# Two MLP layers behind attention: layer 1 of the first half batches cut into two halves of the inner columns

## The chip, the core and the metric

One core of a Trainium2 chip runs the whole program. The metric is the time of one execution on the device in microseconds (us): the median of three runs is 1666.7 us (1664.54 to 1667.3).

## What is computed

Attention with packing, then two gated layers over the 4608 tokens (8 batches of 576, 512 features). The weights come as 64-bit floats, q, k, v and p as 32-bit ones.

```
p_packed = sm_attn(p, k, v)                # 8 batches, 8 heads, 32 packed rows
out      = sm_attn(q, p_packed, p_packed)  # 576 rows per batch
x  = out as [4608, 512]
h  = x @ w_in1                             # 2048 inner columns
g  = (a0 + a1 h + a2 h^2 + a3 h^3) / (1 + |b0||h| + |b1| h^2 + 1e-6)
x2 = g @ w_out1                            # layer 1
h  = x2 @ w_in2;  g = h cos(h)
y  = g @ w_out2                            # layer 2
```

## The kernel before

**Stages.** Attention runs in 16 units (`attention`, a unit is one batch and four heads): loads of p, k, q and v, PE transposes (`trans`, `turned`), scores (`scores`, L500, twice a unit), soft-max on DVE, ACT and POOL, the packing product (`pack`). The packed rows (`keep_pack`) and the attention weights (`keep_attn`) go to DRAM. Layer 1 doesn't form `out`: `m_prod` (L695) multiplies packed rows with `w_in1` into M, per batch, half of the columns and group of heads, and `m_hi`, `m_lo` split M into two parts; `a2_load`, `a2_hi`, `a2_lo` do the same for the attention weights of a half batch (288 tokens).

**Items.** Layer 1 is 128 items: for each of 16 half batches c, eight items i of 256 inner columns. An item is 12 matmuls of `front` (L740) into a PSUM slot b2, some twelve operations for g (ACT: `absolute`, `lin`, `slope`, `log`, `inverse`, `upper`; DVE: `cubic` twice, `over` twice, `ratio`, `lower`; POOL: `denom`), and 24 matmuls of `back` (L777), six into each of four accumulators. After the eighth item `done1` (L786) copies the four to the tile ob and `x_out` stores them. Layer 2 is 144 items: nine chunks of 512 tokens, 16 items each, with `x_load`, `x_hi`, `x_lo` for the operands.

**Weights.** `convert` loads 128 rows of 64-bit words into raw and makes 32-bit values of them: `w_exp`, `w_low` on ACT, `w_abs` (L369), `w_join` (L379) on DVE, and for w_out a split by `w_hi` (ACT) and `w_lo` (POOL).

**What sets the order.** All engines' queues are fixed when the program is built. A planner (`Plan.order`) takes the steps with their costs, keys and slots and puts out one list; a step's key is its due time plus a number for its kind from the table `WANTED`. Slots say how many tiles of a kind live at once:

```
("T", "ep", ("T0", "T1", "T2", "T3")),
...
*((nm, "ld", tuple(f"{nm}_in{i}" for i in range(3))) for nm in "pkqv"),
SLOTS["tr"] = ["b2_0", "b2_1", "b3"]
```

Steps that use DVE's port together with POOL's (`SHARED`: `over`, `ratio`, `lower`, `rounded`, `clipped`, `w_abs`, `w_join`, `x_lo`) are kept apart from POOL's steps: the plan never runs one beside the other, and POOL waits for the last one before it. The pools of layer 1 (`sl2` for M, `a2p`, `ep` for T, U, V) lie in memory that the loads of attention (`ld`) leave, and gh, gl, ob, the accumulators and `wo1` in what its other tiles (`tp`) leave, so the last items' tiles wait for the end of attention (`open_left`, `open_right`). All loads and stores but the last ones go out from SP, in order.

Of the kernel before, what the change touches and what calls it, by code (L numbers as in the profile page):

```python
# [22 lines left out]
class Step:  # L23
    __slots__ = ("eng", "busy", "ns", "key", "fn", "args", "new", "objs", "deps", "outs",
                 "left", "ready", "start", "end", "kb", "n", "slots", "port", "behind", "ins")


class Plan:
# [14 lines left out]
        "a2_hi": -487, "a2_lo": 16, "a2_load": -116, "absolute": -171, "back 0": 868,  # L43
        "back 1": 414, "clipped": -39, "copied k": 50, "copied q": 379, "cosine": 427,
        "cubic 0": 2184, "cubic 1": 373, "denom": -324, "done1": -240, "done2": 222, "doubled": 65,
        "exp1": 12, "exp2": 366, "exp_copied": 1828, "front 0": -75, "front 1": 28, "inverse": -39,
        "keep_attn": -193, "keep_out": -663, "keep_pack": 344, "less_max2": -839, "lin 0": -40,
        "lin 1": -157, "load k": -100, "load p": 127, "load q": -16, "load v": -216, "log": 1940,
        "lower 0": -199, "lower 1": -193, "m_hi": 303, "m_lo": -7, "m_load": -209, "m_prod": -122,
        "max1": 209, "max2": -574, "open_left": 194, "open_right": -121, "over 0": 590,  # L50
        "over 1": 442, "pack": -397, "packed": 485, "ratio": 235, "recip1": 303, "recip2": -376,
        "reduced 0": 499, "reduced 1": 387, "rounded": -296, "scaled2": -170, "scores 0": -545,
        "scores 1": 7, "slope": 61, "store": 293, "sum2": -213, "taken p": 487, "taken pp": -300,
        "times": 372, "trans k": 320, "trans q": -206, "turn2": 432, "turn_back": 314,
        "turn_exp": 342, "turned p": 160, "turned pp": 85, "upper 0": -564, "upper 1": 392,
# [5 lines left out]
        "w_low 1 i": 264, "w_low 1 o": 185, "x_hi": 547, "x_lo": -435, "x_load": 274,  # L61
        "x_out": -308,
    }
    RATE = 262.0
    SHARED = ("over", "ratio", "lower", "rounded", "clipped", "w_abs", "w_join", "x_lo")

    def __init__(self, slots, mixed):
        self.slots_of, self.mixed = slots, mixed
# [4 lines left out]
    def add(self, eng, busy, key, fn, *args, tail=0, r=(), w=(), new=(), after=(), kb=0):  # L73
        key += self.WANTED.get(self.kind(fn.__name__, args), 0)
        s = Step()
        s.eng, s.busy, s.ns, s.key, s.fn, s.args, s.kb = eng, busy, busy + tail, key, fn, args, kb
# [41 lines left out]
    def order(self):  # L118
# [5 lines left out]
        slot_free = {x: 0 for xs in self.slots_of.values() for x in xs}  # L124
# [24 lines left out]
        while len(done) < len(self.steps):  # L149
# [15 lines left out]
            if s.kb:  # L165
                bus = max(bus, a + 600) + s.kb * 1024 / self.RATE
                s.end = bus + 1400
            else:
                s.end = a + s.ns
            if s.eng != "-":  # L170
# [3 lines left out]
                elif s.port:  # L174
                    free["behind DVE"], last = s.end + self.SIGNAL, s
# [26 lines left out]
def pack_attention_moe_moe_kernel(  # L202
# [713 lines left out]
    def nothing():  # L916
        pass
# [194 lines left out]
```

## Time and profile before

| | |
|---|---|
| median of three runs | 1666.7 us |
| the profiled execution, its own time | 1666.77 us |
| its span from first to last instruction | 1665.0 us |
| PE busy | 1577.0 us, 95% |
| DVE / ACT / POOL busy | 1282.2 / 1020.2 / 308.8 us |
| mean granted clock of PE | 0.967 |
| moved by DMA | 120.76 MB |

The slices of the page cut the span into 40 equal parts of 41.6 us, a digit being the busy tenths; the stage tables give busy time of each engine between two times. A matmul's duration overlaps the next one's, so PE's pace is read from a run of matmuls and not from a single row.

### The profile page before, as it was taken

What the parts mean: (1) busy time and instruction counts of PE and PEld (TensorE: products, weight loads), DVE (VectorE), ACT (ScalarE), POOL (GpSimd) and SP (SyncE); (2) the same over time, 40 slices, a digit from 0 to 9 for tenths busy, and PEclk for the clock granted to TensorE, in tenths of its full rate; (3) what the DMA queues carried; (4) which work ended last, traced back from release to release, by engine and by line L of the source; (5) the groups of instructions that cost most, each with busy time, mean ns of one, the idle gap of its engine ahead of it and who ended that gap; (6) DMA issues with size and microseconds to landing.
All of it is one profiled execution on the core that took longest, in us unless ns stands there. A gap on an engine that the chain in (4) does not pass through costs nothing.

```text
span 1665.0 us, 26695 instructions
## 1 busy us (share of the span) xinstructions
PE 1577.0 (95%) x10176; PEld 1353.4 (81%) x10176; DVE 1282.2 (77%) x2025; ACT 1020.2 (61%) x1705; POOL 308.8 (19%) x246
## 2 busy tenths in 40 slices
PE   4877688999999999999999999999999999999998
PEld 3544487999999999999998888888888888888886
DVE  2646988999999999999998766666676657666664
ACT  4655888989898989898977433333333334333332
POOL 0323433333333333333223100000000000000000
PEclk9868688999999999999999999999999999999999
DMA  9897531212112021213244110101010101001010
GB/s 265 243 279 236 137 110 38 67 57 71 53 48 76 29 70 48 76 48 136 77 163 137 36 39 13 39 13 39 8 44 7 43 2 28 23 14 39 1 26 26
DMA packets 84384, 120.76 MB, mean 73 GB/s; under 512 B 19232, under 2 KB 61216, under 8 KB 84256
## 3 DMA queue, kind: packets, MB, share of 16 engines
q1 hardware_dynamic: 83872, 118.53, 24.1%
q8 instruction: 80, 1.31, 0.3%
q10 hardware_dynamic: 384, 0.52, 0.1%
q14 instruction: 48, 0.39, 0.1%
HBM read 85.99 MB, written 33.03 MB: 71 GB/s over the span
## 4 chain that ended last, share of the span: by engine, by line
PE 88%; DVE 4%; ACT 3%; DMA 3%; POOL 1%; issue 1%; SPq 0%; ACTq 0%; POOLq 0%; DVEq 0%
PE acc L777 47%; PE b L756 24%; PE b L740 12%; PE b L695 2%; DMA v_in<-in_v_dram 1%; PE b L471 1%; PE b L500 1%; PE one L551 1%; POOL r L603 0%; DMA raw<-in_moe_w_out_dram 0%; DVE r L578 0%; DMA raw<-in_moe_w_in_dram 0%; POOL r L587 0%; DVE sc L369 0%; PE one L536 0%
## 5 line engine op out<-in xcount | busy, mean ns | idle before, releaser
L777 PE MATMUL acc<-gh,wo 128*128 128x288 f32 x2048 | 419.6, 299 | 4.5 <-ACT gh L903 4.5
L777 PE MATMUL acc<-wo,gh 128*128 128x512 f32 x1152 | 355.3, 390 | 0.0
L777 PEld LDWEIGHTS acc<-gh,wo 128*128 128x128 f32 x2048 | 331.9, 190 | 23.8 <-issue 11.7
L777 PE MATMUL acc<-gl,wo 128*128 128x288 f32 x1024 | 303.3, 296 | 0.3 <-DVE gl L906 0.3
L777 PEld LDWEIGHTS acc<-wo,gh 128*128 128x128 f32 x1152 | 215.7, 188 | 46.0 <-DVE xr L794 1.6
L860 POOL TENSOR_TENSOR U<-U,V 128x576 f32<-128x576 f32 x128 | 182.7, 1439 | 337.7 <-DVE T L875 99.8
L839 ACT ACTIVATE T<-b 128x512 f32<-128x512 f32 x144 | 86.1, 598 | 250.7 <-PE b L756 247.8
L777 PE MATMUL acc<-wo,gl 128*128 128x512 f32 x576 | 224.2, 389 | 0.0
L879 DVE TENSOR_SCALAR T<-T 128x512 f32<-128x512 f32 x144 | 61.3, 426 | 184.3 <-ACT T L839 184.0
L777 PEld LDWEIGHTS acc<-gl,wo 128*128 128x128 f32 x1024 | 194.9, 190 | 0.6 <-DVE gl L906 0.6
L903 ACT CAST gh<-V 128x512 fp32r<-128x512 f32 x144 | 89.5, 622 | 126.0 <-PE acc L777 116.3
L894 ACT ACTIVATE U<-U 128x512 f32<-128x512 f32 x144 | 90.7, 630 | 95.0 <-DVE U L890 94.9
L897 DVE TENSOR_TENSOR V<-U,b 128x512 f32<-128x512 f32 x144 | 98.6, 685 | 36.1 <-ACT U L894 32.2
L777 PEld LDWEIGHTS acc<-wo,gl 128*128 128x128 f32 x576 | 108.1, 188 | 22.5
L906 DVE TENSOR_TENSOR gl<-V,gh 128x512 fp32r<-128x512 f32 x144 | 99.1, 688 | 16.3 <-PE acc L777 15.6
L854 ACT ACTIVATE U<-V,par 128x576 f32<-128x576 f32 x128 | 110.9, 872 | 0.2
L871 DVE SCALAR_TENSOR_TENSOR U<-U,V 128x576 f32<-128x576 f32 x128 | 102.2, 809 | 9.1 <-ACT V L867 8.5
L906 DVE TENSOR_TENSOR gl<-T,gh 128x576 fp32r<-128x576 f32 x128 | 104.0, 815 | 6.1 <-PE acc L777 5.3
L837 ACT ACTIVATE T<-b,par 128x576 f32<-128x576 f32 x128 | 106.4, 833 | 2.7 <-DVE gl L906 2.3
L846 DVE TENSOR_TENSOR T<-T,b 128x576 f32<-128x576 f32 x128 | 93.1, 746 | 12.9 <-ACT T L837 10.9
L848 DVE SCALAR_TENSOR_TENSOR T<-T,par,b 128x576 f32<-128x576 f32 x128 | 101.3, 808 | 1.9
L886 DVE SCALAR_TENSOR_TENSOR U<-T,U 128x512 f32<-128x512 f32 x144 | 100.5, 698 | 2.9
(181 smaller groups left out, 3061.9 us busy)
## 6 DMA issues: line engine op xcount, KB each, us to landing
raw<-in_moe_w_out_dram SPq DMA_DIRECT2D x32, 512.0 KB, 4.2
k_in<-in_k_dram SPq DMA_DIRECT2D x16, 576.0 KB, 5.7
q_in<-in_q_dram SPq DMA_DIRECT2D x16, 576.0 KB, 6.3
x<-ob SPq DMA_DIRECT2D x16, 576.0 KB, 3.4
raw<-in_moe_w_in_dram SPq DMA_DIRECT2D x32, 256.0 KB, 4.3
v_in<-in_v_dram SPq DMA_DIRECT2D x64, 128.0 KB, 5.8
raw<-in_moe_w_in_dram SPq DMA_DIRECT2D x16, 512.0 KB, 4.4
w<-sc SPq DMA_DIRECT2D x32, 256.0 KB, 2.5
```

The source lines that it names most:

```text
L740: nc.tensor.matmul(TILE["h", j][:, e, 0:HS], lhsT=w[:, o : o + P], rhs=x[:, g, :], start=n == 0, stop=n == 3 * NG - 1,)
L756: nc.tensor.matmul(h, lhsT=w[:, ks], rhs=x, start=n == 0, stop=n == 3 * KC - 1)
L777: nc.tensor.matmul(o, lhsT=w, rhs=x, start=i == 0 and n == 0, stop=i == last and n == len(todo) - 1,)
L837: nc.scalar.activation(T, hidden(j), AF.Identity, scale=par[:, 3:4], bias=par[:, 2:3])
L846: nc.vector.tensor_tensor(T, T, h, op=ALU.mult)
L848: nc.vector.scalar_tensor_tensor(T, T, par[:, 1:2], h, op0=ALU.add, op1=ALU.mult)
L854: nc.scalar.activation(shaped(j, "U"), shaped(j, "V"), AF.Identity, scale=par[:, 5:6], bias=par[:, 4:5])
L860: return nc.gpsimd.tensor_tensor(Q, Q, V, op=ALU.mult)
L871: return nc.vector.scalar_tensor_tensor(t, t, add_, shaped(j, "V"), op0=ALU.add, op1=ALU.mult)
L886: return nc.vector.scalar_tensor_tensor(Y, T, -C2, Y, op0=ALU.mult, op1=ALU.add)
L897: nc.vector.tensor_tensor(shaped(j, "V"), shaped(j, "U"), hidden(j), op=ALU.mult)
L906: return nc.vector.tensor_tensor(shaped(j, "gl"), result(j), shaped(j, "gh").bitcast(F32), op=ALU.subtract)
```

## The change

The first eight half batches (`CE = 8`, four batches) are no longer done with all eight items in one go. Their items are grouped in halves: first the items i = 0 to 3 (inner columns 0 to 1023) of the half batches 0 to 7, 32 items, which need only the first eight pieces of `w_in1` and of `w_out1` and the units of their own batch; then items 4 to 7 of the same half batches, and then the other half batches with eight items each as before. The first half's result and the second half's go to DRAM apart, and layer 2 loads both (`x_load`, `x_rest`) and adds them on POOL (`x_sum`) ahead of the split.

So that early items can live beside attention, memory is laid out anew: M of the first half, a2, T, U, V, gh, gl, ob and two accumulators have places of their own from the start, the loads p, k, q, v get two slots each and no longer three, the transposed attention weights two and not nine, and PSUM's slot b3 goes, so that attention's transposes and scores share b2 with the fronts. An early item has two accumulators: its backs for m = 0, 1 run first, `done1` copies them, and the backs for m = 2, 3 follow for the four items of the group (`late`), with four slots each of gh and gl. The keys become a start and a step per group of steps (`FIRST`, `EACH`), the table `WANTED` has new numbers, and a transfer's cost in the plan is a time and no longer a size.

```diff
+    CE = 8
...
-        *((nm, "ld", tuple(f"{nm}_in{i}" for i in range(3))) for nm in "pkqv"),
+        *((nm, "ld", tuple(f"{nm}_in{i}" for i in range(2))) for nm in "pkqv"),
...
-        ("a2T", "tp", tuple(f"a2T{i}" for i in range(9))),
+        ("a2T", "tp", tuple(f"a2T{i}" for i in range(2))),
...
+    for pool, home, tags in (("acc", "aps2", ("acc2", "acc3")), ("gh", "gx", ("gh3",)), ("gl", "gx", ("gl2", "gl3"))):
+        SLOTS[pool, "E"] = list(SLOTS[pool])
+        SLOTS[pool if pool == "acc" else (pool, "E")] += tags
...
-    SLOTS["tr"] = ["b2_0", "b2_1", "b3"]
+    SLOTS["tr"] = ["b2_0", "b2_1"]
...
-    items = [(0, c, i) for c in range(NH) for i in range(NPR)]
+    HALF = NPR // 2
+    groups = [(c, a) for a in range(2) for c in range(CE)] + [(c, a) for c in range(CE, NH) for a in range(2)]
+    items = [(0, c, a * HALF + i) for c, a in groups for i in range(HALF)]
...
+    def x_rest(c, kk):
+        for done, hc, s, n in halved(c):
+            nc.sync.dma_start(
+                TILE["xq", c, kk][:, done : done + n], x2[1][hc][kk * P : (kk + 1) * P, s : s + n]
+            )
+
+    def x_sum(c, kk):
+        done, _, _, n = halved(c)[-1]
+        xr = TILE["xr", c, kk][:, 0 : done + n]
+        return nc.gpsimd.tensor_tensor(xr, xr, TILE["xq", c, kk][:, 0 : done + n], op=ALU.add)
...
+                sets[b, n] = 0 if c < CE and n == 0 else (len(sets) - CE // 2 + 1) % 2
...
+        backs((0, 1) if early else range(KC), i)
+        if i == last:
+            if early:
+                ended((0, 1))
+                for n in range(first, last + 1):
+                    backs((2, 3), n, " late")
+            ended((2, 3) if early else range(KC))
```

What it adds: eight more groups with four `done1` each (96 and not 64), eight more `a2_load`, `a2_hi`, `a2_lo`, 16 more `m_load`, eight more `x_out`, 20 `x_sum` with their loads. The matmuls are the same in number.

**PE, where the first front of layer 1 stands.** Before, at the end of attention, behind the last units' work (b are PSUM slots; L500 scores, L487 a transpose, L695 `m_prod`, L740 `front`):

```order
L500 MATMUL b_1_2258<-qT_2137,lhpp_2236 32x288 x8
L487 MATMUL one_2278<-ident,pp_2167 128x128
L695 MATMUL b_0_2287<-s_586,pt_766 32x512 x2
L695 MATMUL b_0_2287<-s_929,pt_766 32x512 x2
L740 MATMUL b_1_2314<-a_0_2233,m00h 128x288 x2
L740 MATMUL b_1_2314<-a_0_2233,m00l 128x288
L740 MATMUL b_1_2314<-a_0_2233,m01h 128x288 x2
L740 MATMUL b_1_2314<-a_0_2233,m01l 128x288
```

Now, between two units' transposes and packing (L493 `trans`, L558 and L560 `turn_exp`, L573 `pack`, L769 `front`):

```order
L558 MATMUL one_1165<-ident,e_1_1113 128x128 x4
L560 MATMUL one_1175<-ident,e_1_1113 32x128 x2
L493 MATMUL b_1_1179<-ident,q_in_910 128x128 x5
L493 MATMUL b_0_1188<-ident,q_in_910 128x128 x4
L769 MATMUL b_1_1204<-a_0_1130,m00h 128x288 x2
L769 MATMUL b_1_1204<-a_0_1130,m00l 128x288
L769 MATMUL b_1_1204<-a_0_1130,m01h 128x288 x2
L769 MATMUL b_1_1204<-a_0_1130,m01l 128x288
L573 MATMUL one_1225<-v_in_960,e1T_1125 32x64 x20
L769 MATMUL b_0_1252<-a_0_1130,m00h 128x288 x2
```

Before, 31 of the 32 score steps stand ahead of the first front; now 14. The third front stands there too, the fourth behind 18 score steps, and the ninth is the first behind all of them.

**DVE, in the second half of attention.** Before, it has soft-max steps of two units in turn (L560 `packed`, L594 and L583 reductions, L578 and L606 transposes):

```order
L560 TENSOR_SCALAR pp_2008<-one_2007,sm_1699 128x128
L594 TENSOR_REDUCE mx_1963<-r_1962 128x18
L578 STREAM_TRANSPOSE r_2037<-b_1_2036 128x576
L598 TENSOR_SCALAR mx_1963<-mx_1963 128x18
L599 RECIPROCAL mx_1963<-mx_1963 128x18
L583 TENSOR_REDUCE mx_2038<-r_2037 128x18
L545 COPY e1T_2054<-one_2071 64x128
L606 STREAM_TRANSPOSE a2T_2080<-r_1962 128x576
```

Now a layer-1 item's `cubic` (L893, L895) and a conversion (L398, L408) stand between them:

```order
L893 TENSOR_TENSOR T_1952<-T_1952,b_0_1921 128x576
L567 COPY e1T_1947<-one_1969 64x128
L600 STREAM_TRANSPOSE r_1957<-b_1_1956 128x576
L628 STREAM_TRANSPOSE a2T_2009<-r_1760 128x576
L398 SCALAR_TENSOR_TENSOR sc_2007<-sc_1983,sc_2007 128x512
L605 TENSOR_REDUCE mx_1958<-r_1957 128x18
L582 TENSOR_SCALAR pp_1986<-one_1985,sm_1813 128x128
L895 SCALAR_TENSOR_TENSOR T_1952<-T_1952,par,b_0_1921 128x576
L408 SCALAR_TENSOR_TENSOR sc_2007<-raw_1774,sc_2007 128x512
```

Between the third item and the ninth, DVE's list has ten of the units' last steps (L628), 12 conversions and six items.

**SP, the first loads.** Before, three tiles of a kind are filled ahead (the digit behind `k_in` is the slot):

```order
L455 DMA k_in0_192<-in_k_dram 128x1152
L455 DMA k_in1_194<-in_k_dram 128x1152
L455 DMA k_in2_196<-in_k_dram 128x1152
L455 DMA q_in0_198<-in_q_dram 128x1152
L455 DMA q_in1_200<-in_q_dram 128x1152
L455 DMA q_in2_202<-in_q_dram 128x1152
```

Now two, and the third k load (into `k_in0` again) has to wait for the first unit's transposes:

```order
L477 DMA k_in0_218<-in_k_dram 128x1152
L477 DMA k_in1_220<-in_k_dram 128x1152
L477 DMA q_in0_222<-in_q_dram 128x1152
L477 DMA q_in1_224<-in_q_dram 128x1152
L372 DMA raw0_237<-in_moe_w_in_dram 64x512 x2
L372 DMA raw1_242<-in_moe_w_in_dram 64x512 x2
L465 DMA p_in0_254<-in_p_dram 128x64
L465 DMA p_in1_257<-in_p_dram 128x64
L477 DMA k_in0_272<-in_k_dram 128x1152
```

All loads of attention behind these wait their turn on the same queue.

## Rows read from the trace of the kernel before

**Rows 1.** The page's slices of 41.6 us, a digit is busy tenths.

```profile
PE   4877688999999999999999999999999999999998
DVE  2646988999999999999998766666676657666664
POOL 0323433333333333333223100000000000000000
PEclk9868688999999999999999999999999999999999
DMA  9897531212112021213244110101010101001010
```

**Rows 2.** Stages: us, busy (x instructions) by engine, PEclk, DMA share, GB/s.

```profile
0.00:156.00 156.00, 104.68 (x1443) 69.02 (x1447) 79.85 (x176) 89.81 (x183) 36.90 (x50) 0.85 0.95 267
...
79.00:184.00 105.00, 77.69 (x954) 48.89 (x946) 64.66 (x129) 63.36 (x125) 38.56 (x38) 0.72 0.81 231
...
177.00:229.00 52.00, 38.21 (x240) 32.95 (x239) 46.71 (x71) 41.97 (x66) 19.79 (x16) 0.78 0.47 137
229.00:358.00 129.00, 119.80 (x897) 112.27 (x898) 120.17 (x163) 116.15 (x186) 46.45 (x34) 0.93 0.18 57
```

**Rows 3.** Timeline of PE: start us, us, what, count, idle before it.

```profile
78.55 0.67 PE L500 MATMUL b<-qT,lhpp 64*32 64x288 f32 x12
...
176.56 0.85 PE L740 MATMUL b<-a,m00h 128*128 128x288 f32 x2
...
183.33 0.72 PE L500 MATMUL b<-qT,lhpp 64*32 64x288 f32 x16
...
229.05 0.50 PE L740 MATMUL b<-a,m00h 128*128 128x288 f32 x2 [1.48 <-DVE T L848]
```

**Rows 4.** The chain that ended last: start us, us, piece; layers 1 and 2.

```profile
275.64 3.20 PE b L740 x24
...
1040.69 5.44 PE b L756 x24
```

**Rows 5.** Groups of DVE: busy us, mean ns of one, idle before.

```profile
L906 DVE TENSOR_TENSOR gl<-T,gh 128x576 fp32r<-128x576 f32 x128 | 104.0, 815 | 6.1 <-PE acc L777 5.3 <-ACT gh L903 0.3
L871 DVE SCALAR_TENSOR_TENSOR U<-U,V 128x576 f32<-128x576 f32 x128 | 102.2, 809 | 9.1 <-ACT V L867 8.5
L871 DVE SCALAR_TENSOR_TENSOR T<-T,par,V 128x576 f32<-128x576 f32 x128 | 101.7, 810 | 0.0
L848 DVE SCALAR_TENSOR_TENSOR T<-T,par,b 128x576 f32<-128x576 f32 x128 | 101.3, 808 | 1.9
...
L875 DVE SCALAR_TENSOR_TENSOR T<-U,T 128x576 f32<-128x576 f32 x128 | 94.5, 751 | 0.2
L846 DVE TENSOR_TENSOR T<-T,b 128x576 f32<-128x576 f32 x128 | 93.1, 746 | 12.9 <-ACT T L837 10.9 <-ACT V L851 1.0 <-PE acc L777 0.7
...
L369 DVE SCALAR_TENSOR_TENSOR sc<-sc,sc 128x512 uint32<-128x512 uint32 x64 | 47.5, 742 | 19.8 <-ACT sc L363 17.0 <-ACT sc L360 2.5
```

**Rows 6.** Groups of ACT, the same columns.

```profile
L863 ACT ACTIVATE V<-U 128x576 f32<-128x576 f32 x128 | 86.4, 686 | 18.6 <-POOL U L860 18.1
...
L360 ACT ACTIVATE sc<-raw 128x512 f32<-128x512 f32 x64 | 43.3, 677 | 13.9 <-DMA raw<-in_moe_w_in_dram 6.4 <-DMA raw<-in_moe_w_out_dram 6.0 <-DVE sc L369 0.9
...
L786 ACT ACTIVATE ob<-acc 128x288 f32<-128x288 f32 x64 | 26.3, 413 | 4.7 <-PE acc L777 4.5
...
L682 ACT CAST a<-xr 128x576 fp32r<-128x576 f32 x16 | 10.7, 672 | 0.0
```

**Rows 7.** Groups of POOL, the same columns.

```profile
L860 POOL TENSOR_TENSOR U<-U,V 128x576 f32<-128x576 f32 x128 | 182.7, 1439 | 337.7 <-DVE T L875 99.8 <-DVE T L871 85.0 <-ACT gh L903 46.0
...
L391 POOL TENSOR_TENSOR sc<-sc,sc 128x512 fp32r<-128x512 f32 x16 | 20.8, 1302 | 22.4 <-issue 6.4 <-ACT T L837 4.3 <-DVE U L871 4.1
```

**Rows 8.** DMA: a landing time in us by issue group; SP's last q load.

```profile
xr<-x SPq DMA_DIRECT2D x32, 144.0 KB, 2.3
...
151.13 0.38 SPq L455 DMA_DIRECT2D q_in<-in_q_dram  x1
```

More of the change, by code (lines that the diff above doesn't have):

```diff
@@ L969, in operands1 @@
-                    add("DVE", 1140, key, m_lo, b, a, g, tail=85, r=[("mps", b, a, g), ("M", b, a, g, "h")], w=[("M", b, a, g, "l")])
-        add("SP", 120, first - 60, a2_load, c, r=[("a2 out", b * NG + g) for g in range(NG)], new=[("xr", ("a2r", c), [P, NG, HS], F32)], kb=290, after=[fronts[NPR * (c - 1)]] if c > 1 else ())
-        add("ACT", 570, first - 20, a2_hi, c, tail=100, r=[("a2r", c)], new=[("a2", ("a2", c), [P, 2, NG, HS], F32R)], after=opened_at("a2"))
-        add("POOL", 1395, first - 20, a2_lo, c, r=[("a2r", c)], w=[("a2", c)])
+                    add("SP", 60, at(j + n * HALF, -50), m_load, b, n, g, r=[("kept", b * NG + g)], new=[(f"pt{g}", ("PT", b, n, g), [P, P], F32)], bus=320)
@@ new lines, in operands1 @@
+        if a == 0 or c < CE:
+            x = half(c, a * HALF)
+            add("SP", 120, at(j, -60), a2_load, c, x, r=[("a2 out", b * NG + g) for g in range(NG)], new=[("xr", ("a2r", c, x), [P, NG, HS], F32)], bus=880, after=[fronts[j - 7]] if j > 7 else ())
+            add("ACT", 570, at(j, -20), a2_hi, c, x, tail=100, r=[("a2r", c, x)], new=[("a2", ("a2", c, x), [P, 2, NG, HS], F32R)])
+            add("POOL", 1435, at(j, -20), a2_lo, c, x, r=[("a2r", c, x)], w=[("a2", c, x)])
+    early_users = []
@@ L974, in item1 @@
     def item1(j):
         l, c, i = items[j]
+        early = c < CE and i < HALF
+        pool = (lambda x: (x, "E")) if early else (lambda x: x)
+        a = half(c, i)
         key = at(j)
-        ep = opened_at("T")
-        M = [("M", c // 2, i // 4, g, e) for g in range(NG) for e in "hl"]
-        fronts[j] = add("PE", 1600, key, front, j, tail=170, r=[("a2", c), *M], new=[("b2", ("h", j), *ps2)], after=[fronts[j - 1]] if j else ())
-        add("ACT", 545, key, absolute, j, tail=95, r=[("h", j)], new=[("V", ("V", j), *W2P)], after=ep)
@@ L981, in item1 @@
-        add("ACT", 730, key, lin, j, tail=100, r=[("h", j)], new=[("T", ("T", j), *W2P)], after=ep)
-        add("ACT", 760, key, slope, j, tail=105, r=[("V", j)], new=[("U", ("U", j), *W2P)], after=ep)
+        M = [("M", c // 2, i // HALF, g, e) for g in range(NG) for e in "hl"]
+        fronts[j] = add("PE", 1600, key, front, j, tail=170, r=[("a2", c, a), *M], new=[("b2", ("h", j), *ps2)], after=[fronts[j - 1]] if j else ())
+        add("ACT", 545, key, absolute, j, tail=95, r=[("h", j)], new=[("V", ("V", j), *W2P)])
@@ new lines, in item1, with backs @@
+        if early:
+            early_users.extend((u, w))
+        first, last = ends(c, i)
+        def backs(ms, i, late=""):
+            k = j - items[j][2] + i
+            for m in ms:
+                home = dict(w=[("acc", 0, c, a, m)]) if i > first else dict(new=[(pool("acc"), ("acc", 0, c, a, m), [P, CH], F32)])
+                s = add("PE", 800, key, back, k, m, tail=170, r=[("gh", k), ("gl", k), ("wo", 0, 2 * i), ("wo", 0, 2 * i + 1)], late=late, **home)
+                if early:
+                    early_users.append(s)
@@ L1004, in operands2 @@
             if c == 0:
[L1005 removed]
+                key, after = (lambda off, n=n: at(N1 - 4 + n, off)), [fronts[N1 - 6 + n]]
             else:
```

311 lines of the change are left out of this document (172 added, 139 removed), and 11 rows, old and new, of the table WANTED.

## The prediction, with its working

> **What bounds the kernel now.** Read first the slices of the span [rows 1]. From the eighth slice on PE's digit is 9 and its granted clock is full: there the time is PE's, whatever DVE and ACT do. Ahead of that lie some 290 us in which PE has gaps and a granted clock of 0.6 to 0.9, and in the first four slices the DMA engines are at 7 to 9 tenths, while DVE and ACT are half idle. The stage table [rows 2] gives it in numbers: in the first 156 us DMA is busy 0.95 of the time and DVE 79.85 us of 156. From 229 to 358 us PE is busy 119.80 of 129. Last the timeline of PE [rows 3], for four marks: the 14th of the 32 score steps (two to each attention unit) ends at 79.2 us, the first layer-1 front starts at 176.56, the last score step at 183.33, and the ninth front (first of the second half batch) at 229.05, 1.48 us late for DVE's L848. A layer-1 item is 36 matmuls (12 of `front`, 24 of `back`), and the chain has 24 in 3.20 us [rows 4]: 0.133 us each, 4.8 us an item.
>
> **The yardstick.** I count what stands in PE's queue ahead of the ninth front. Before: all 16 attention units, eight fronts, four `m_prod` and the backs of four items. In the change: the same units, fronts and products, and the backs of four and a half items. What PE has left after its ninth front is thus equal to within 12 matmuls (1.6 us), and from there PE was all but saturated. So the gain is how much earlier the ninth front starts, less what the stages behind it lose.
>
> **When the third front can start.** The change's first three fronts stand behind 14 score steps, so seven units. Those ended at 79.2 us [rows 3]. SP carries the same eight `w_in` pieces ahead of that point and one more k load: 0.59 MB at 267 GB/s [rows 2], 2 us. The two first fronts took 176.56 to 183.33 [rows 3], 6.8 us, at a low clock. 79 + 2 + 7 gives 88, and I write 90.
>
> **From the third front to the ninth.** Here the change puts six items beside the other nine units. In the kernel before the same nine units lie between 79 and 184 us, and in that stretch DVE was busy 64.66 us, ACT 63.36, PE 77.69 at clock 0.72 [rows 2]. Added on DVE, by the order's counts and the mean of each operation [rows 5]: 6 L846 (746 ns) and 6 L848 (808), 16 L871 (some 810), 7 L875 (751), 6 L906 (815), together 32.4 us; two more conversions (four operations like L369, 742 ns) 3.0; off go 1.6 for the two operations of the first item that the old stretch held. 64.7 + 32.4 + 3.0 - 1.6 = 98.5 us. DVE has kept 46.71 of 52 us busy (0.90, from 177 to 229) and 120.17 of 129 (0.93) where items and conversions mix [rows 2]; at these shares 98.5 us take 106 to 109, and I take 107. ACT gets six operations an item of like length on its 63.36, and ends some 8 us below DVE. PE gets 72 front and some 108 back matmuls: 24 us at full clock, 33 at 0.72. Its 77.69 then become 80 (all of it at full clock) to 111 (none), about the same length as DVE's. The ninth front comes at 90 + 107 = 197 us, 32 earlier than 229.05.
>
> **Behind the ninth front.** To the 32nd item before took 129 us [rows 2] with PE at 0.93. There the order gives the change 8 more L786 (413 ns), 4 more L682 (672) and some 7 conversion operations (677) on ACT, and some 7 operations fewer like L863 (686) [rows 6]: 3.3 + 2.7 + 4.7 - 4.8, about 5 us (with one L704 fewer still 5). ACT was at 116.15 of 129 there [rows 2], so I charge all 5. Ends of this cost: nothing, if ACT's gaps take it, and 10 us. The same stretch rewrites the first half's M in one set of slots, without a spare, and each group of four items holds its gh and gl until the late backs: for both PE has backs to run in the meantime, and the 10 us stand for what they leave. Later, up to the 128th item, ACT gets 20 more L786 and 3 more L682, 10 us on 490, under a saturated PE: nothing.
>
> **Layer 2.** Twenty `x_sum` on POOL have no row. They lie between L391 (1302 ns, 128x512) and L860 (1439, 128x576) [rows 7]; I take 1.3 by shape, 26 us on an engine whose digits are 0 there [rows 1]. For each operand the chain load, sum, split grows by one load (2.3 us to landing) [rows 8] and 1.3. The latest of these loads is let go two fronts ahead of its use, and two items are 24 matmuls of front and 24 of back, 5.44 us each [rows 4], 10.9 us: covered, nothing. Without that cover five chunk changes of 3.6 us would cost 18. The eight extra stores and loads of half sums are 9.4 MB in stages where DMA is at 0 to 5 tenths: nothing. Closing and opening pools at other points and the new keys issue no instruction.
>
> **Fewer buffers.** k, q, v and p have two slots in place of three, transposes and scores two PSUM slots in place of three, which the fronts now share. SP takes its waits in order: a k load that waits for `trans` of two units before holds every load behind it. I charge nothing, because the first pair lands earlier and SP is free of `w_in` for the second half; the other end is rival (a).
>
> **Sum.** 1666.8 (the profiled execution; 1665.0 us span and 1.8 around it, and 0.1 above the median of 1666.7) - 32 + 5 = **1640 us**.
>
> **Rivals.**
> (a) *Attention starves on two slots.* For it: the last q load went out at 151.13 us [rows 8] only because DMA ran at 0.95 with three slots, and 33 us of attention followed to the end of the last score step. Against it: nine units took 105 us, so with two slots one is filled again only every 23 us. At a DMA share of 0.70 the 156 us become 212, the ninth front comes at 212 + 33 = 245, and the time is 1666.8 + 16 + 5 = 1688. It decides from a share of about 0.76 on, where the ninth front comes at 224.
> (b) *DVE and POOL exclude each other.* POOL was busy 38.56 us from 79 to 184 [rows 2] and gets six L860 more, 47 us. If nothing of DVE ran beside them, the stretch would be 98.5 + 47 = 146 us, the ninth front at 236, and the time 1666.8 + 7 + 5 = 1679. But from 229 to 358 DVE's 120.17 and POOL's 46.45 add to 167 in 129 us, so at least 38 of POOL's 46 us ran beside DVE [rows 2]. What can still wait are the operations that the planner's SHARED list keeps apart from POOL's: 53 here (24 of conversion, 29 of items). Meeting POOL with chance 47 / 107 and waiting half an L860, that is 17 us: ninth front at 214, time 1657. The Trainium skill, SBUF — State Buffer, section "SBUF: two separate sides", has the narrow form: an exclusive lock, taken by DVE operations that read two SBUF operands and by GpSimd, with the loser blocked for the whole instruction. By that rule this change, which packs more POOL work into DVE's fullest stretch, is worth 10 us and not 27; the trace agrees that the wide form is wrong, and no row shows how often the narrow one bites.
> (c) *The items are free.* If PE's clock rises with its new work and DVE fills to 0.98, the old pace of attention rules: ninth front right behind the last score step, at 184, nothing given back, 1666.8 - 45 = 1622.
> That the change does not do what it says can't be: the queues' order is fixed, and six fronts stand inside the attention.
>
> **How the numbers follow.** What a measurement here can tell from no change is 0.2%, 3.3 us. Forecast, 1630 to 1650: 0.55. (c): 0.12. (b), narrow: 0.18. (a) and the wide (b), which are slower: 0.15, of which 0.03 end within 0.2%, and 0.02 of the narrow (b) too. Faster 0.83, same 0.05, slower 0.12. The range goes from 1622 (case c) to 1672 (ninth front no earlier, 5 us given back); beyond lie most of (a) and little else.
>
> **What would show it.** Right: the ninth front near 197 us; DVE at 0.9 or more from 90 to 197; DMA near 0.95 up to some 155 us; from the ninth front to the 32nd item 130 to 140 us; layer 2 as long as before, with no gap of PE at a chunk's first front. Wrong: waits of PE for k or q loads between 20 and 150 us (a); DVE operations of L871's kind at twice their length beside POOL (b); PE idle beyond 1 us at the changes of M, or in front of layer 2's chunks, which would make the 5 us too small.

## The result, and the profile after

| | before | after |
|---|---|---|
| median of four runs each, us | 1665.6 (1662.2 to 1667.3) | 1646.6 (1646.1 to 1648.3) |
| ratio to before, 95% interval | | 0.9890 (0.9872 to 0.9909) |
| the profiled execution, its span | 1666.8, 1665.0 | 1648.3, 1646.5 |
| PE / DVE / ACT / POOL busy | 1577.0 / 1282.2 / 1020.2 / 308.8 | 1564.8 / 1289.8 / 1036.8 / 343.1 |
| mean granted clock | 0.967 | 0.989 |
| moved by DMA, MB | 120.76 | 133.63 |

The change makes the kernel 19 us faster, 1.1%; forecast were 27 (1640, range 1622 to 1672). The sign and the place of the gain are as forecast. Two terms of the sum were not, and their errors point in opposite directions.

The page's slices after, to be held against [rows 1]:

```profile
PE   4677899999999999999999999999999999999998
DVE  3588999899999999999899876666666667676664
POOL 1154334334343343333322200000000000000000
PEclk9899999999999999999999999999999999999999
DMA  9899732212223121215344320201010101001010
```

PE reaches its 9 two slices earlier, DVE has 8 in the third and fourth slices where it had 4 and 6, and the fourth and fifth slices of DMA are 9 and 7 where they were 7 and 5: what stood behind attention now stands beside it.

The stages after, which answer to [rows 2] (busy us and instructions of PE, PEld, DVE, ACT, POOL, then PEclk, DMA share, GB/s):

```profile
0.00:156.00 156.00, 105.19 (x1392) 69.65 (x1392) 99.37 (x191) 105.09 (x203) 51.24 (x60) 0.92 0.92 246
...
89.00:192.00 103.00, 86.34 (x1148) 62.66 (x1149) 90.11 (x164) 87.10 (x165) 51.61 (x48) 0.95 0.90 249
192.00:321.00 129.00, 115.78 (x845) 107.82 (x844) 119.30 (x169) 117.06 (x194) 44.46 (x32) 0.96 0.32 96
321.00:493.00 172.00, 168.82 (x1315) 160.11 (x1315) 159.50 (x213) 157.80 (x259) 65.82 (x47) 1.00 0.21 68
...
820.00:931.00 111.00, 106.38 (x537) 90.75 (x538) 103.62 (x161) 76.02 (x129) 32.37 (x25) 1.00 0.46 141
```

The same view of before, for the two stages that the last two rows answer to (items 32 to 64, and the 128th front to the second chunk of layer 2):

```profile
358.00:522.00 164.00, 163.99 (x1286) 156.15 (x1285) 156.00 (x212) 147.74 (x236) 59.10 (x42) 1.00 0.19 60
...
848.00:947.00 99.00, 99.00 (x497) 84.75 (x496) 86.25 (x145) 64.69 (x111) 22.63 (x17) 1.00 0.34 113
```

Before, PE has no idle time in these. After, it has 3.2 and 4.6 us. The PE timeline after, at the third front, the last score step, the ninth front and the 128th, beside [rows 3]:

```profile
94.03 0.37 PE L769 MATMUL b<-a,m00h 128*128 128x288 f32 x1 [0.48 <-DVE T L895]
...
184.85 0.72 PE L522 MATMUL b<-qT,lhpp 64*32 64x288 f32 x16
...
192.33 0.43 PE L769 MATMUL b<-a,m00h 128*128 128x288 f32 x2
...
820.19 0.50 PE L769 MATMUL b<-a,m00h 128*128 128x288 f32 x2 [0.29 <-DVE T L895]
```

The starts of all such marks, each from the same timeline, tell where the gain arises and where it goes:

| mark | before, us | after, us | gain |
|---|---|---|---|
| last score step | 183.33 | 184.85 | -1.52 |
| 9th front | 229.1 | 192.3 | 36.7 |
| 32nd front | 357.7 | 321.2 | 36.5 |
| 64th front | 522.1 | 492.8 | 29.3 |
| 128th front | 848.2 | 820.2 | 28.0 |
| first front of layer 2 | 854.7 | 830.2 | 24.5 |
| first front of its second chunk | 947.4 | 931.1 | 16.3 |
| last matmul of `back` | 1658.1 | 1641.3 | 16.8 |

A mark alone misleads where the order has put more or less work ahead of it. At 0.133 us a matmul [rows 4], the change has 12 more matmuls of backs done at the ninth front, 24 fewer at the 32nd, 36 fewer at the 128th, and 6 more (of layer 2, 0.227 us each) at the second chunk; at the 32nd it also has one `m_prod` of some 1 us fewer done. So the true losses are about 6 us from the ninth to the 32nd front (36 backs and one product less done in the same 129 us), 9 up to the 128th (8.5, with 12 backs less and the one product more done), and 6 up to the second chunk (11.7 us lost, of which 42 backs more, 6 us, are only work that stands later). From the second chunk to the last matmul of `back` layer 2 takes 710.2 us, and 710.7 before.

### The profile page after: what moved, and what is told of

It reads as the page before. It is cut to its first block, busy times and chain, and to the rows that moved or that the text cites. A ratio compares the mean times of both kernels' runs of the same rounds, so it can differ in the third digit from the quotient of the medians.

```text
span 1646.5 us, 26978 instructions
## 1 busy us (share of the span) xinstructions
PE 1564.8 (95%) x10176; PEld 1340.0 (81%) x10176; DVE 1289.8 (78%) x2025; ACT 1036.8 (63%) x1745; POOL 343.1 (21%) x274
## 2 busy tenths in 40 slices
DMA packets 100130, 133.63 MB, mean 81 GB/s; under 512 B 22176, under 2 KB 76960, under 8 KB 100000
## 4 chain that ended last, share of the span: by engine, by line
PE 77%; ACT 8%; DVE 7%; DMA 5%; issue 2%; SPq 1%; POOL 0%; DVEq 0%; ACTq 0%; POOLq 0%
PE acc L806 41%; PE b L785 23%; PE b L769 9%; DMA raw<-in_moe_w_in_dram 2%; PE b L719 2%; DVE T L893 1%; DMA raw<-in_moe_w_out_dram 1%; ACT T L884 1%; DMA v_in<-in_v_dram 1%; DVE T L895 1%; DVE U L918 1%; PE b L493 1%; DVE T L922 1%; DVE T L918 1%; ACT V L898 1%
## 5 line engine op out<-in xcount | busy, mean ns | idle before, releaser
L806 PEld LDWEIGHTS acc<-gh,wo 128*128 128x128 f32 x2048 | 328.2, 188 | 25.5 <-issue 16.6
L907 POOL TENSOR_TENSOR U<-U,V 128x576 f32<-128x576 f32 x128 | 182.5, 1435 | 369.3 <-DVE T L922 107.7
L926 DVE TENSOR_SCALAR T<-T 128x512 f32<-128x512 f32 x144 | 62.3, 433 | 189.7 <-ACT T L886 189.0
L806 PEld LDWEIGHTS acc<-wo,gl 128*128 128x128 f32 x576 | 108.2, 188 | 22.4
L884 ACT ACTIVATE T<-b,par 128x576 f32<-128x576 f32 x128 | 106.3, 830 | 16.8 <-PE b L769 14.8
L953 DVE TENSOR_TENSOR gl<-T,gh 128x576 fp32r<-128x576 f32 x128 | 108.8, 853 | 9.1 <-PE acc L806 4.5
L933 DVE SCALAR_TENSOR_TENSOR U<-T,U 128x512 f32<-128x512 f32 x144 | 105.4, 732 | 3.4
L895 DVE SCALAR_TENSOR_TENSOR T<-T,par,b 128x576 f32<-128x576 f32 x128 | 101.0, 808 | 7.8 <-ACT V L898 6.5
L893 DVE TENSOR_TENSOR T<-T,b 128x576 f32<-128x576 f32 x128 | 92.9, 745 | 15.8 <-ACT T L884 8.2
```

The lines of the kernel that those rows point to most:

```text
L806: nc.tensor.matmul(o, lhsT=w, rhs=x, start=i == first and n == 0, stop=i == last and n == len(todo) - 1,)
L884: nc.scalar.activation(T, hidden(j), AF.Identity, scale=par[:, 3:4], bias=par[:, 2:3])
L893: nc.vector.tensor_tensor(T, T, h, op=ALU.mult)
L895: nc.vector.scalar_tensor_tensor(T, T, par[:, 1:2], h, op0=ALU.add, op1=ALU.mult)
L907: return nc.gpsimd.tensor_tensor(Q, Q, V, op=ALU.mult)
L933: return nc.vector.scalar_tensor_tensor(Y, T, -C2, Y, op0=ALU.mult, op1=ALU.add)
```

## The experiments

Four questions: what sets the ninth front, what the halves themselves are worth, what takes the later 16 us, and whether DVE and POOL stop each other. One measure recurs: the **excess** of the SHARED operations (and of `reduced`), summed from the trace's single records as each one's time above the length that a fifth of its line and shape stay under; the expectations' words for it are loose. Times of runs are medians; a profile shows one execution. Queues that no edit had touched up to there ended the 14th score step at 78 to 85 us in different executions, so stages are compared by their length, not by their start. Diffs are cut to what bears on the reading; `...` marks a cut.

**DVE's work taken out of the early items.**

```diff
     for s in plan.order():
+        if (s.fn.__name__, s.args[1:]) in (("cubic", (1,)), ("over", (0,)), ("ratio", ())) and s.args[0] < 9:
+            s.ins = None
+            continue
...
-        if s.port and s.eng == "POOL" and s.behind:
+        if s.port and s.eng == "POOL" and s.behind and s.behind.ins:
```

The last line belongs to all three edits that leave DVE's steps out: where the step that POOL's guard waits for is left out, POOL waits for none.

> Leaves out three DVE operations of g (the second cubic, the over on T, the ratio) in the first nine items; the queues' order stays. For the six items between the third front and the ninth that is 6 times 0.81, 0.74 and 0.75, 14 us of the 94.94 that DVE is busy from 89 to 197 us. Theory T (the prediction's sum: DVE's work at its share sets the length of this stretch): the ninth front comes 10 to 15 us earlier than 192.3, at 177 to 182, and the last score step earlier than 185 too; time 1632 to 1638. Rival F (the attention's own feed sets it, the loads at a DMA share of 0.90, and the items fill gaps): last score step 183 to 186, ninth front 189 to 193, time 1643 to 1648.

Measured: 1646.6 (1645.0 to 1648.6), ratio 0.9888 (0.9873 to 0.9904), the change's own. Last score step at 182, third front at 87.6, ninth at 189.7. The stage table of this kernel:

```profile
89.00:192.00 103.00, 84.83 (x1082) 61.46 (x1080) 75.81 (x143) 84.33 (x160) 48.13 (x44) 0.88 0.87 240
```

DVE lost 14.3 us of its 90.11 and the stretch from the third front to the ninth took 102.1 us, not less than the change's 98.3. Theory T falls, if the clock doesn't hide it: the granted clock is 0.88 here and 0.95 in the change. The other executions with this order, but for the one with more loads, took 97.8 to 100.4 us at 0.95, 99.8 and 100.1 at 0.93, and 100.7 at 0.92. By these lengths, as an estimate, the lower clock may hide some 5 us, and not the 10 to 15 of Theory T.

**More loads in the same stretch.**

```diff
...
+            if nm == "k" and u >= 7:
+                nc.sync.dma_start(spare[u], src[b, hs].rearrange("h (p c) d -> (h p) c d", c=2 * NT9))
```

> Every k load from the eighth unit on is issued a second time, into a DRAM tile that nobody reads: 9 times 0.59 MB, 5.3 MB, at 246 GB/s 21.6 us of the DMA engines' time, between some 70 and 150 us. Nothing else changes. Theory F (the loads set the pace of the stretch from 89 to 192 us): the last score step moves from 185 to 200 or later, the ninth front to 205 to 214, the time to 1658 to 1669. Rival T (DVE's work sets it): the 0.08 of DMA's time that were free take up 8 us of the 21.6, the rest delays loads whose units wait for DVE anyway; last score step 185 to 192, time 1646 to 1654.

Measured: 1658.2 (1654.1 to 1661.6), 12 us over the change; last score step at 191, ninth front at 198.7.

```profile
89.00:192.00 103.00, 79.63 (x1030) 57.30 (x1029) 79.62 (x148) 78.20 (x149) 43.05 (x43) 0.90 0.94 271
```

The time lies at the lower end of F, the score step at the upper end of T: neither number alone decides. The ninth front, too, comes before F's 205. The loads matter, as DVE's work does not, but with slack: part of the 21.6 us went into the share (0.90 to 0.94) and into the rate (249 to 271 GB/s), and some 6 us (ninth front) to 12 us (time) came through. So the loads on SP's queue, attention's and the weights', set part of the pace here. The chain that ended last in the change says the same; three of its longest pieces between the third front and the ninth are

```profile
98.20 9.28 DMA raw<-in_moe_w_out_dram
...
120.01 10.15 DMA v_in<-in_v_dram
130.23 5.91 DMA p_in<-in_p_dram
```

Summed over that chain from 94 to 192 us, loads are 35 us, all of it ahead of 156 us, PE 27, ACT 16 and DVE 15. Before, from 79 to 183 us, loads are only 7 us of the chain, PE 32, DVE 32, POOL 14 and ACT 14.

**The early start undone, the halves kept.**

```diff
-after=[fronts[j - 1]] if j else ())
+after=[fronts[j - 1]] if j else [s for s in plan.steps if s.fn is scores])
...
-        convert(1, f, "o", at(N1 + f), after=[fronts[min(n, N1 - 1)]])
+        convert(1, f, "o", at(N1 + f), after=[fronts[min(n, N1 - 1)], *last_i])
```

> The change with one thing undone: the first front waits until PE has done all 32 score steps, so no item runs beside attention; halves, late backs, sums, slots and the tables stay, and the planner makes its order anew (the w_out conversions of layer 2 are also held until the last w_in conversion, without which the planner finds no order). In the change the first front starts between 83 and 89 us and the ninth at 188 to 192; in the kernel before at 176.6 and 229.0. Theory E (the early items are the whole gain, and the halves alone cost some 10 to 20 us): last score step 180 to 186, first front 183 to 190, ninth front 220 to 235, time 1665 to 1690. Rival A (the new layout and tables make attention itself faster): last score step 170 to 178, ninth front 205 to 218, time 1645 to 1662.

Measured: 1727.8 (1727.5 to 1728.2). Last score step at 181, first front at 181.6, ninth at 230.7, as E has them (the first front 1 us earlier), and 128th at 854.0 (848.2 before, 820.2 in the change). The time is outside both ranges, for the most part by something else: from there the first two chunks of layer 2 take 129.7 and 102.5 us (100.9 and 80.5 in the change), with these waits of PE from 859 to 1092 us:

```profile
PE b L785 <- DVE V L944: 24.6, 11, 3.8
PE acc L806 <- ACT wo L415: 12.9, 1, 12.9
```

That the tables do not fit the order that the planner makes here, and that the added hold delays w_out, is how I read these waits; no run separates the two. Up to the 128th front the change is 34 us ahead and the kernel before 6. With the backs counted (24 more done here than in the change, 12 fewer than before) the early start is worth 31 us and the halves alone cost 7, of which the misfit of the tables may be a part.

**The halves undone, the early start kept.**

```diff
-    CE = 8
+    CE = 0
...
-                sets[b, n] = 0 if c < CE and n == 0 else (len(sets) - CE // 2 + 1) % 2
+                sets[b, n] = 0 if c < CE and n == 0 else len(sets) % 2
```

(and the `xp` pool opens when attention's tiles are gone).

> The change with CE = 0: the layout, the slots, the tables and the early start stay, but every half batch is done with its eight items in one go (no halves, no late backs, no sums), M of the two halves takes the two sets of slots in turn, and the planner makes its order anew. M of the second half lies in memory that the end of attention leaves. Theory H (halving is what makes enough items ready during attention): only four items can run early, the fifth front comes behind the last score step at 185 to 195 and the ninth at 203 to 220, time 1654 to 1670. Rival L (the early start of the first four is what counts, and halving only adds copies and sums): ninth front 195 to 203, time 1640 to 1650.

Measured: 1710.3 (1708.5 to 1711.9). Fourth front at 111.1, fifth at 200.5, ninth at 214.1, 128th at 859.6. PE's waits from 190 to 300 us:

```profile
PE acc L806 <- POOL wo L420: 14.8, 4, 7.8
PE b L769 <- ACT V L898: 9.0, 2, 6.4
```

H holds for the marks up to the ninth front: four items can run early and the fifth stands behind attention, later even than H has it. Its time is again out of range. Layer 2's first two chunks (105.4 and 99.5 us) lose 24 us against the change; 39 stand at the 128th front already. The ninth front is 15 us earlier than before, but from there to the 32nd it takes 143.2 us (128.7 before), in waits such as the two above, and at the 128th front no gain is left. The tables were searched for halves, so what four early items would be worth with tables of their own is open.

**POOL's guard taken away.**

```diff
-        if s.port and s.eng == "POOL" and s.behind:
+        if s.port and s.eng == "POOL" and s.behind and False:
```

> POOL no longer waits for the last SHARED operation of DVE ahead of it; the queues' order and all waits for data stay. In the changed kernel, from 89 to 197 us, 8 of 62 SHARED operations have POOL beside them, for 3.4 us, and last 2.7 us longer for it, while the other DVE operations have POOL beside them for 34.3 us and last 0.3 longer. Theory L (DVE operations of the SHARED kinds stand still while POOL works): without the guard POOL falls upon them by chance, some 128 L907 of 1.44 us with a chance of 0.45 and about half an operation each, 40 us of DVE time, of which a third to two thirds shows in layer 1 where DVE is at 0.92 to 0.95: 1657 to 1672 us, and the excess of the SHARED operations from 89 to 820 us rises from some 23 us to 50 or more. Rival N (the longer durations are chance and the guard only delays POOL): 1640 to 1647.

Measured: 1709.8 (1706.5 to 1711.2), ratio 1.0265: 63 us slower than the change, beyond L's 1672, and N falls. From 89 to 820 us the excess is 77.0 us (23.0 in the change); 199 SHARED operations have POOL beside them for 166.8 us and lose 75.5, while the other DVE operations, with at most one SBUF input, have it beside them for 139.9 us and lose 0.9 (SBUF and PSUM are the core's two memories; the tiles b and acc lie in PSUM, most others in SBUF). Two DVE groups and POOL's, from 321 to 493 us, first of the change:

```profile
L895 DVE SCALAR_TENSOR_TENSOR T<-T,par,b 128x576 f32<-128x576 f32 x32 | 25.1, 808 | 2.4 <-ACT V L898 2.2
L922 DVE SCALAR_TENSOR_TENSOR T<-U,T 128x576 f32<-128x576 f32 x32 | 23.8, 750 | 0.1
...
L907 POOL TENSOR_TENSOR U<-U,V 128x576 f32<-128x576 f32 x33 | 47.0, 1435 | 93.3 <-DVE sc L408 26.2 <-DVE gl L953 26.0 <-DVE T L918 17.4
```

and of the kernel without the guard:

```profile
L922 DVE SCALAR_TENSOR_TENSOR T<-U,T 128x576 f32<-128x576 f32 x30 | 31.4, 1056 | 0.1
...
L895 DVE SCALAR_TENSOR_TENSOR T<-T,par,b 128x576 f32<-128x576 f32 x28 | 22.1, 808 | 2.5 <-ACT V L898 2.2
...
L907 POOL TENSOR_TENSOR U<-U,V 128x576 f32<-128x576 f32 x29 | 49.6, 1712 | 98.3 <-ACT U L901 94.9 <-DVE gl L953 3.3
```

L922 reads T and U, both in SBUF, and goes from 750 to 1056 ns; L895 reads b from PSUM and stays at 808. POOL's own operation pays as well, 1435 to 1712: by the same measure POOL's operations lose some 58 us from 89 to 820 us (2 in the change).

**The sums left out.**

```diff
     for s in plan.order():
+        if s.fn.__name__ in ("x_rest", "x_sum"):
+            continue
```

> Leaves out the twenty loads x_rest and the twenty x_sum of layer 2, so the second half's part of the sum is missing for the first eight half batches; every queue keeps its order otherwise. The change gains 36.7 us at the ninth front and 18.5 at the end of the profiled execution (1648.3 for 1666.8). From the first front of layer 2 to that of its second chunk it takes 100.9 us where the kernel before takes 92.7, and there the DVE operations that the planner calls SHARED, with POOL beside them for 21.6 us, last 10.1 us longer in sum than the fifth shortest of their kinds in a hundred ordered by length would say (3.4 us before, with 10.4 us of POOL beside them). Theory S (the sums on POOL hold up DVE): that excess falls to 3 to 6 us, the second chunk's first front comes 4 to 7 us earlier (924 to 927), the time is 1640 to 1643. Rival C (the later w_out conversions of layer 2 are to blame, three pieces more behind the 128th front): the second chunk's front moves by less than 1.5 us, time 1645 to 1647. My prediction's own step (the sums cost nothing) says the same as C for the time.

Measured: 1642.6 (1642.3 to 1646.2). The excess from 820 to 931 us falls from 10.1 to 6.4, but the second chunk's first front stands 110.3 us behind the 128th, against 110.9: S falls by the trace, though the time is S's. So it was run again, beside the unedited change on one chip:

> The kernel without x_rest and x_sum once more, now beside the unedited change (it leaves out the second half's part of layer 2's operands). The first run was 4 us below the change, but on another chip, and of those 4 us 3.9 stood at the ninth front already, before any sum. Theory S (the sums hold up DVE): 3 to 5 us below the unedited change. My prediction's step (the sums are covered): at most 1.5 us below it.

> The changed kernel itself, without an edit, beside the next three on one chip: 1645 to 1648. Its stretches show how far two executions of the same queues differ: the first 14 score steps ended at 84 us in the change's profiled execution and at 78 to 81 in four kernels with the same queues up to there, so I expect 78 to 84, and the later stretches within 1 us of the first ones.

Measured side by side: 1644.9 (1643.6 to 1646.2) without the sums, 1646.5 (1641.5 to 1651.2) with them; from the 128th front to the second chunk 111.4 and 113.1 us. The medians are 1.6 us apart, near the prediction's 1.5 and below S's 3, and the runs do not tell that from nothing.

The unedited kernel's own expectation held for its time and its 14th score step (81.8 us), and failed for the stretches: from the third front to the ninth it took 100.7 us here and 98.3 in the first execution, and from the first front of layer 2 to its second chunk 103.1 and 100.9. Differences of 2 us in these stretches mean nothing.

**Layer 2's conversions.** First the w_in conversions let go earlier:

```diff
-    KEEP1, KEEPN = 40, 5.2
+    KEEP1, KEEPN = 40, 4.6
```

> The conversions of layer 2's w_in come every 4.6 items from the 40th front on and no longer every 5.2, so the last of the 16 is let go at the 109th front and not at the 118th; the planner makes its order anew. In the change three conversions more than before are left behind the 128th front, and from the first front of layer 2 to that of its second chunk it takes 100.9 us where the kernel before takes 92.7, with DVE at 0.93. Theory C (these late conversions are what that stretch loses): it takes 94 to 97 us, PE's idle time there falls from 3.6 us to under 2, time 1640 to 1644. Rival D (DVE is as full ahead of it, and what is moved forward is lost there): the stretch shortens as under C, but the 128th front comes 3 to 6 us later than at 816 to 820, time 1645 to 1650.

Measured: 1650.6 (1648.5 to 1653.9); 128th front at 819.7, and 103.1 us from the first front of layer 2 to its second chunk. C falls, and D too: nothing shortened, the 128th front is no later, and the time is just above D's range. Then DVE's part of the w_out conversions left out:

```diff
     for s in plan.order():
+        if s.fn.__name__ in ("w_abs", "w_join") and s.args[::2] == (1, "o"):
+            s.ins = None
+            continue
...
```

> Leaves out the DVE operations w_abs and w_join in the conversion of layer 2's w_out (16 pieces, 32 operations of 0.69 us, 22 us of DVE's time), so layer 2 gets wrong weights; the queues' order stays. Between the first front of layer 2 and that of its second chunk the change has DVE at 0.93, and 17 pieces are converted from the 128th front on. Theory C (DVE's work is what that stretch loses): it takes 92 to 96 us in place of 100.9, time 1637 to 1642. Rival W (it is the weights' way through the loads, ACT and POOL, or PE's own work): 99 to 101 us, time 1644 to 1647.

Measured: 1642.6 (1640.1 to 1644.8), the stretch 98.3 us in place of 100.9, between the two theories.

```profile
820.00:931.00 111.00, 108.90 (x545) 92.81 (x545) 85.95 (x130) 75.18 (x129) 35.25 (x26) 1.00 0.45 141
```

PE's idle time there falls from 4.6 us to 2.1, with DVE at 0.77 and no longer at 0.93. So in this execution DVE's fullness is about half of what PE idles here, not all of it; the four executions that have the change's order and all of its work there took 100.9 to 103.1 us for the stretch. The excess did not fall (10.8 us from 820 to 931, 10.1 in the change), so the time beside POOL is not what was won.

**DVE's work taken out of the middle.**

```diff
+        if (s.fn.__name__, s.args[1:]) in (("over", (0,)), ("ratio", ())) and 32 <= s.args[0] < 128:
+            s.ins = None
+            continue
...
```

> Leaves out two DVE operations of g (the over on T and the ratio) in the 33rd to the 128th item, 192 operations of 0.74 to 0.81 us, 150 us of DVE's time; the queues' order stays. In the change PE waits from the 32nd front to the 128th for some 7 us, most of it for the PSUM slot that the second cubic (L895) gives back late, where the kernel before waits for nothing. Theory D (DVE is late there, its time and its stops beside POOL): these waits fall to under 2 us, the 32nd front to the 128th takes 488 to 493 us in place of 499, time 1637 to 1642. Rival P (it is PE's own order, with one more group's products and copies in between): 497 to 500 us, time 1644 to 1648.

Measured: 1640.6 (1635.5 to 1645.2), but the 32nd front to the 128th took 497.9 us and not under 493. The stage, and PE's waits from 321 to 820 us, the first row of the change, the others of this run:

```profile
321.00:493.00 172.00, 168.86 (x1318) 160.55 (x1317) 125.87 (x158) 157.59 (x259) 67.75 (x47) 1.00 0.21 68
```

```profile
PE b L769 <- DVE T L895: 3.2, 7, 1.0
...
PE b L769 <- DVE T L895: 3.9, 9, 1.0
PE b L719 <- PE acc L806: 1.5, 2, 0.8
PE b L719 <- issue: 0.5, 1, 0.5
```

With DVE at 0.73 in place of 0.93 PE's busy time is the same to 0.04 us. The change's seven waits for L895 stand here too, within 1.1 us of their old places. P holds for this stretch in the profiled execution. But the median time is D's, not P's, and the profiled execution was the slowest of the four (1645.2): where the lower median comes from the trace can't show, and its interval (0.9824 to 0.9872) meets the unedited kernel's (0.9864 to 0.9906). Nor did the edit remove the stops beside POOL, D's other half: with guards dropped the excess from 321 to 820 us rose from 17 to 34 us. Yet between the kernel before and the change it hardly differs: 15 us before, from 358 to 848, and 17 after.

**A version of my own.**

```diff
-s.eng, s.busy, s.ns, s.key, s.fn, s.args, s.bus = eng, busy, busy + tail, key, fn, args, bus
+s.eng, s.busy, s.ns, s.key, s.fn, s.args, s.bus = eng, busy, busy + tail, key, fn, args, bus * 1.15
```

with other numbers in `WANTED`, `FIRST` and `EACH`.

> A version of my own: the change with every transfer 1.15 times as long in the plan, so that the plan's score steps come when the trace has them (the last at 182 us), and with the three tables searched anew under that cost. Theory G (the plan drifts from the chip because it takes the loads as too short, so DVE and POOL meet where the plan keeps them apart): the excess of the SHARED operations from the third front to the 128th falls from 22 or 23 us to under 15, time 1632 to 1642. Rival K (the drift has other causes, and the order is as good as such an order gets): excess 18 to 28 us, time 1643 to 1656.

Measured: 1636.9 (1632.6 to 1637.0), ratio 0.982 (0.980 to 0.984): faster than both kernels, 9.6 us below the unedited change on the same chip. The excess is 22.4 us, unchanged, so G's mechanism falls although its time came; K has the excess right and the time wrong. The gain is made by the 32nd front (309.8, and 321.0 in the unedited kernel beside it); from there to the 128th it takes 501.5 us, and the unedited one 498.5. Its last score step stands at 196.2, behind the ninth front (187.7) and not at the 182 that it was made for. Up to the 32nd front PE is at 0.93 (0.90 in the change), and PE does not wait for the rewrite of M there (3.5 us in the change; here 1.9 us come later, at 368 us):

```profile
188.00:321.00 133.00, 123.22 (x953) 113.14 (x952) 124.09 (x175) 123.37 (x202) 51.25 (x37) 0.99 0.33 99
```

The cost and the tables were changed together, so which of them did it is open.

## Why the prediction was right, and where it was wrong

**Bound and yardstick: right.** PE was the bound behind attention, and what moved the end was how early the ninth front came, less losses behind it. The late start and the undone halves speak for both halves of the idea: without either, the 128th front stands at 854 to 860 us, with tables that were searched for the change's order, which may be a part of it.

**Third front at 90: right.** 94.0 in the profiled execution, 87.6 to 92.1 in the nine others with the same order up to there.

**Third front to ninth, 107 us: the step that failed first.** It made DVE's work the length of the stretch. The work was sized well (98.5 forecast from 90 to 197 us; 94.94 from 89 to 197), its role was not: 14.3 us less of it brought no gain. The stretch took 98.3 us, at a DVE share of 0.87. By the chain it was held by loads up to 156 us (DMA 0.92) and then mostly by PE's own queue (24 of 36 us). That isn't what the same units waited for before, when loads were 7 of 104 us of the chain: the items filled gaps of every engine, and the loads came up behind them. The last score step came only 1.5 us later than before, so six items went in almost free. This is rival (c)'s mark with a remainder, though DVE did not fill to 0.98: the ninth front stands 7 us behind the last score step, since two `m_prod` and 30 matmuls of the early items' backs are queued between. The granted clock rose from 0.72 to 0.95, as (c) supposes; what part of the gain that is, no run isolates. The forecast erred by 5 us, on the safe side.

**Behind the ninth front, 5 us: near in size for its stretch, wrong behind it.** Up to the 32nd front the loss was 6 us. PE's longest waits from 192 to 321 us, and of before from 229 to 358 us:

```profile
PE b L769 <- DVE T L895: 6.1, 4, 2.6
PE b L769 <- DVE m01l L732: 3.5, 1, 3.5
PE acc L806 <- ACT gh L950: 1.9, 2, 1.1
```

```profile
PE b L740 <- ACT V L851: 4.0, 1, 4.0
PE b L695 <- ACT V L851: 2.7, 1, 2.7
```

The second row of the change is the rewrite of M, the third a late gh: the two places that the prediction named beside ACT's work. But PE waited 12.8 us there in all and 10.6 before, so these rows are not a loss in full, and that ACT's 5 us were the cause is not shown. Then came "later, up to the 128th item, nothing under a saturated PE", and this is the term that was mis-sized: 9 us were lost there. PE idles 7.3 us in this stretch and 0.3 before; 6.3 are ten waits of over 0.3 us, of which there are none before, chiefly for the b2 slot that L895 gives back, and for `m_prod`. In the profiled execution of the middle run the waits stayed with DVE at 0.73, so there DVE's load is not the cause. At five of the seven waits for L895 the trace shows a chain: DVE starts `cubic` within 0.6 us of the end of `lin`, and the second `cubic` within 0.8 us of the end of the first, and PE's next instruction is the front that waits for the slot. PE was saturated by an order that had backs at hand, and the new one does not at these places. That the order is to blame is argued from them; no run isolates it, and my own version, whose gain lies ahead of the 32nd front, does not speak for it.

**Layer 2, nothing: right for the sums, wrong for the entry.** From the second chunk on it took as long as before (710.2 and 710.7 us), and without the sums the kernel is 1.6 us faster by the medians, within the noise. But 6 us went between the 128th front and the second chunk, 4.6 as PE's idle time. About half of that is DVE at 0.93, which converts w_out later. It also meets POOL more often (excess 10.1 us, 3.4 before), but no run shows a cost of that here. The rest is open: earlier w_in conversions did not help.

**The rivals.** (a), starving on two slots, happened only in small: DMA's share stayed at 0.90 to 0.92, and PE's waits for k and q loads from 20 to 150 us, the sign that was named, are 7.4 us (none before, 2.5 in the change's second profile). The doubled k loads show that the slack was thin. In (a)'s working a share of 0.76 gives a ninth front at 228 us and not at 224; nothing hangs on it. (b) in its narrow form is true as a mechanism and was priced too high: from 89 to 197 us the excess was 2.7 us, not 17, because the prediction let POOL meet the SHARED operations by chance, and the plan's guard prevents most of it over the whole kernel. Without the guard it becomes the largest cost of all, 63 us, though in this stretch it is even then only 5.8 us of excess: the 63 arise behind the ninth front, which stands at 191.3 us there. The Trainium skill, SBUF — State Buffer, section "SBUF: two separate sides", says that a DVE operation with two SBUF inputs and a GpSimd operation that reads SBUF exclude each other for a whole instruction. The rows above agree, in which operations lose (L922, not L895) and in that both sides pay: 75.5 us and some 58 us of the 166.8 that they stand side by side.

**The signs.** Of those named as right, three came out otherwise: DVE at 0.88 from 90 to 197 us and not at 0.9 or more, DMA at 0.92 and not near 0.95, and 129 us from the ninth front to the 32nd item and not 130 to 140. Of those named as wrong, two came beside (a)'s: PE idle for 3.5 us at a rewrite of M, and up to 1.7 us in one wait at the entry of layer 2.

**The sum again:** 36.7 gained at the ninth front, 38 with the backs done there; 6, 9 and 6 lost; 2 regained behind the last matmul of `back`: 19, where the forecast had 32 less 5. That 19 came near 27 is in part luck: the ninth front came 5 us earlier than forecast, and 15 us were lost in places that had been priced at nothing.

## What to carry to other kernels

Work that is moved beside a stage in which every engine has gaps can cost that stage little, even where an engine's busy time seems to add up to its whole length: ask what sets the stage now, and add to that. The price came later here, in a saturated engine whose new order no longer had spare work at hand between two dependent steps; "saturated, so nothing" was read from the old order and held only for it. And where a planner keeps two engines apart, measure what it prevents before pricing the collision by chance.

## What the runs showed of the chip

- DVE operations with two SBUF inputs and POOL's operations lengthen each other (L922 from 750 to 1056 ns, L907 from 1435 to 1712); a guard on one side alone, in a fixed order, is worth 63 us here.
- The DMA engines were not at their limit at a share of 0.90: the same stretch carried 271 GB/s with more loads queued (share 0.94), and 249 without.
- The granted clock in attention rose from 0.72 [rows 2] to 0.95 with the items beside it. From the third front to the ninth the unedited change took 98.3 us at 0.95 and 100.7 at 0.92; which follows from which is not shown.
- Identical queues differ by 6 us at the 14th score step from one execution to the next, by 2 us from the third front to the ninth, and by about 1 us from the 32nd to the 128th.
